# Turning maxima and gate sums from tiles of 128 columns, and a new order of the first steps

## The chip, the cores and the metric

The kernel runs on one core of one Trainium2 chip. The metric is the device time of one execution in microseconds; the median of three timed runs counts. The engines are named as in the profile: PE multiplies matrices (PEld loads its stationary operand, the weights), DVE, ACT and POOL work on vectors, SP issues most of the transfers. Each engine and each queue works its instructions off in order; between engines, semaphores keep the order of the data.

## The reference, cut to what matters

```python
def _attn_ref(q, k, v, proj):            # 4 x 8 heads, 768 tokens, 64 wide; 6 hash bits
    q_bits = (np.einsum('bhsd,dk->bhsk', q, proj) > 0).astype(np.int64)
    k_bits = (np.einsum('bhsd,dk->bhsk', k, proj) > 0).astype(np.int64)
    mask = q_bucket[:, :, :, None] == k_bucket[:, :, None, :]
    scores = scale * np.matmul(q, k.transpose(0, 1, 3, 2))
    scores = np.where(mask, scores, -1000000000.0)
    scores = scores - np.max(scores, axis=-1, keepdims=True)
    attn = np.exp(scores)
    attn = attn / (np.sum(attn, axis=-1, keepdims=True) + 1e-09)
    return np.matmul(attn, v).astype(np.float32)

def _moe_ref(x, w_gate, w1, w2, capacity):   # x: 4 x 768 x 512, capacity 128
    scores = np.einsum('bsd,d->bs', x, w_gate)
    for b in range(B):
        top_idx = np.argpartition(-scores[b], capacity)[:capacity]
        ye = np.maximum(x[b, top_idx] @ w1, 0.0) @ w2
        g = 1.0 / (1.0 + np.exp(-scores[b, top_idx]))
        out[b, top_idx] = x[b, top_idx] + g[:, None] * ye
    return out
```

Queries and keys fall into buckets by the signs of six projections; a query attends to the keys of its bucket. Of each batch's 768 tokens the 128 with the largest gate sums go through a small network.

## The kernel before, in words

The whole program is one list of steps, ORDER (lines 44 to 172). A step is a name with numbers, as `mx.5.1.2`; the loop at L1014 calls the function of that name, which issues its instructions. Each engine gets its instructions in the order in which the list names them, and a semaphore wait is set by what was listed before. The string BANKS says which of four PSUM tiles each step takes that asks for one: big (L260) gives 1024 columns, two banks, one (L263) gives 512. One more bank holds the sums av.

One head h (32 of them) goes through these steps.

- X loads q and k with the 64 features on partitions, xh and xl split them into two 16-bit parts, h or hx multiplies by the projections (32-bit for heads 0 to 3), sg or sx takes the signs. For head 0 the signs are taken straight from PSUM (hash_direct L331, signs_direct L342): hx is one tile of two banks, half e of the tokens in bank e, and sx.0.i.e reads half e for i, queries or keys.
- pa, ps and pb place the parts in the tiles A (queries and keys with their sign rows) and B, as transfers on SP, of which da, dd and xq are the forms for head 0. kd takes differences of key thirds (halves in head 0).
- mx, re and rd find each query's maximum: max_unit (L523) adds a product to a PSUM tile, re makes it non-negative on ACT, then the next product is added, and rd takes the largest on DVE.
- mq (max_clamp, L554) clamps the maxima of all 768 queries into a tile of 128 x 6 in 16 bits; mt (max_turn, L559) turns that on PE into 6 x 128; mc copies it out on DVE; mr places it as a row of A by a transfer. Heads 0 and 1 go another way: mk clamps (clamp_part, L575), mu (row_turn, L581) multiplies each single column with the identity, and mv copies the row.
- s (L619 and L622) multiplies keys by queries in five units, e takes the exponential on ACT, r the low part on DVE, a (L703) multiplies by the values, six steps of 18 products each; w puts the first sums into av, rc and n divide.

After eight heads of a batch, sc sums x times the gate weights on DVE into one column for each 128 tokens (score, L738; the tile of the second half of the features is sct[b, 1], 128 x 6 in 32 bits). tp (turn_scores, L788) turns it to 6 x 128 on PE, ty, ts and sb spread it over the partitions. For the last batch bp (L770) does that on PE in two halves of one PSUM tile, and bc (L783) copies the halves, bc.0 on ACT and bc.1 on DVE. lt, ow, cl, cw and se count ranks, ip, ix and ga gather the chosen tokens, tx, hi and lo turn them, up, hh, hl and dn are the network, fi and sr write back.

wa (warm_av, L658) multiplies a tile of ones by itself into columns of av that nobody reads: its first number is a label, its second the count. init_rest (L287) fills constants on POOL; i0 fills the tile of ones, iv fills constant columns of V and W. wa.0.30 stands near the head of the list.

Of the kernel before, what the change touches and what calls it, by code (L numbers as in the profile page):

```python
# [59 lines left out]
mx.5.1.0 re.5.1.0 re.4.1.1 a.2.4 mx.4.0.2 wl.0.1 rd.4.0 mx.5.0.0 a.2.5 mx.4.1.2 s.3.0 rc.2 rd.4.1 vh.2 n.2 re.5.0.0  # L60
vs.3 mx.5.1.1 e.3.0 X.12 re.5.1.1 s.3.2 e.3.2 wl.0.0 ps.6.0 pb.4.2 w.3 xl.10 X.9 mq.4 mt.4 mc.4 ps.7.0 vw.3 pb.4.3
s.3.1 pb.6.2 mx.5.0.1 pb.6.3 pb.5.0 e.3.1 mx.5.1.2 wt.1 pa.7.1 vl.2 s.3.3 xh.9 s.3.4 mr.4 e.3.3 r.3.0 xh.11 pa.7.0
a.3.0 a.3.1 V.4 kd.6 mx.6.0.0 pb.7.2 r.3.1 X.13 a.3.2 a.3.3 pb.6.0 xl.9 pb.4.1 e.3.4 re.5.0.1 mx.5.0.2 r.3.2 xl.11
pb.7.3 a.3.4 re.6.0.0 a.3.5 wh.1 xh.12 rd.5.0 rd.5.1 wl.1.1 ps.7.1 lg mx.6.0.1 h.2.0.4 mq.5 re.6.0.1 sg.2.0.4 pb.5.1
ws.3 wc.3 mx.6.1.0 re.6.1.0 mt.5 mc.5 pa.8.0 xl.12 X.14 mr.5 X.15 xh.13 rc.3 mx.6.0.2 rd.6.0 vs.4 mx.6.1.1 s.4.0
ps.8.0 re.6.1.1 mx.6.1.2 rd.6.1 e.4.0 pb.6.1 xl.13 s.4.2 s.4.3 s.4.4 vh.3 e.4.2 pa.8.1 n.3 vr.2 sc.0.0.0 e.4.3 w.4
s.4.1 e.4.1 pb.7.1 ps.8.1 r.4.0 s.5.0 mq.6 sc.0.0.1 e.4.4 s.5.2 kd.7 r.4.1 a.4.0 a.4.1 e.5.0 po.0 pb.7.0 mx.7.0.0
mx.7.1.0 re.7.0.0 re.7.1.0 mt.6 a.4.2 a.4.3 vl.3 r.4.2 V.5 mc.6 mr.6 sc.0.0.3 mx.7.0.1 mx.7.1.1 pb.8.2 e.5.2 a.4.4
a.4.5 re.7.1.1 kd.8 re.7.0.1 sc.0.0.4 s.5.1 e.5.1 wl.1.0 pa.9.0 pb.8.3 rc.4 s.5.3 mx.7.0.2 wt.2 pa.9.1 ps.9.1 s.5.4
pa.10.0 vw.4 n.4 pb.9.2 mx.7.1.2 r.5.0 r.5.1 pa.10.1 w.5 vs.5 a.5.0 a.5.1 pb.9.3 e.5.3 rd.7.0 rd.7.1 e.5.4 xh.14 s.6.0  # L70
e.6.0 mx.8.1.0 r.5.2 re.8.1.0 vr.3 X.16 ps.9.0 s.6.2 a.5.2 mq.7 e.6.2 ps.10.0 vw.5 a.5.3 a.5.4 a.5.5 rc.5 wh.2 xl.14
vh.4 mt.7 mc.7 mx.8.0.0 re.8.0.0 mr.7 n.5 r.6.0 pb.8.1 vl.4 s.6.1 sc.0.0.5 w.6 mx.8.1.1 re.8.1.1 pb.9.0 pb.9.1 kd.9
vr.4 wl.2.1 mx.8.0.1 V.6 a.6.0 ws.4 a.6.1 re.8.0.1 wl.2.0 mx.8.0.2 mx.8.1.2 pb.8.0 wc.4 e.6.1 xh.15 rd.8.0 rd.8.1 mq.8
r.6.1 s.6.4 s.7.0 ps.10.1 X.17 e.7.0 s.6.3 pb.10.2 e.6.3 pb.10.3 s.7.2 e.7.2 lc pa.11.1 mx.9.0.0 a.6.2 mt.8 mc.8 vs.6
mr.8 pa.11.0 a.6.3 e.6.4 wt.3 re.9.0.0 s.7.1 ps.11.1 s.7.3 s.7.4 pa.12.1 e.7.1 pb.11.2 pb.11.3 mx.9.1.0 r.6.2 r.7.1
pb.10.0 pb.10.1 e.7.3 mx.9.0.1 re.9.1.0 a.6.4 a.6.5 mx.9.1.1 r.7.0 xl.15 X.18 rc.6 re.9.0.1 n.6 xh.16 xl.16 mx.9.0.2
rd.9.0 s.8.0 re.9.1.1 mx.9.1.2 rd.9.1 mq.9 w.7 a.7.0 s.8.2 e.7.4 e.8.0 sc.0.0.2 xh.17 a.7.1 kd.10 mt.9 mc.9 e.8.2
pb.11.1 a.7.2 r.7.2 a.7.3 ws.5 kd.11 mr.9 wh.3 wc.5 X.21 mx.10.0.0 re.10.0.0 s.8.1 e.8.1 ps.11.0 r.8.0 a.7.4 mx.10.0.1
re.10.0.1 wl.3.1 pa.12.0 X.19 a.7.5 rc.7 n.7 wl.3.0 vh.5 xl.17 s.9.0 mx.10.0.2 e.9.0 w.8 rd.10.0 s.8.3 e.8.3 vl.5
mx.10.1.0 re.10.1.0 sc.0.1.0 wt.4 h.3.0.4 V.7 s.8.4 e.8.4 pa.13.1 pa.13.0 sg.3.0.4 vw.6 ps.12.1 sc.0.1.3 r.8.1 s.9.2  # L80
pb.12.3 a.8.0 mx.10.1.1 a.8.1 e.9.2 sc.0.1.2 mx.11.1.0 r.8.2 re.10.1.1 re.11.1.0 mx.11.0.0 re.11.0.0 sc.0.1.5
mx.10.1.2 rd.10.1 sc.0.1.4 po.1 a.8.2 s.9.1 xh.18 mx.11.0.1 mq.10 e.9.1 re.11.0.1 ps.13.1 a.8.3 vr.5 mt.10 sc.0.1.1
a.8.4 mc.10 mr.10 tp.0 ty.0 ts.0 ps.12.0 r.9.0 ps.13.0 pb.11.0 a.8.5 rc.8 n.8 wh.4 mx.11.1.1 sb.0 pb.12.2 vs.7 vw.7
mx.11.0.2 rd.11.0 re.11.1.1 s.9.4 s.9.3 pb.13.2 pb.13.0 mx.11.1.2 rd.11.1 mq.11 w.9 a.9.0 r.9.1 pa.14.0 e.9.3 e.9.4
# [971 lines left out]
```

## Time and profile before

| | |
|---|---|
| median of three runs | 391.91 us (391.43 to 393.45) |
| profiled execution, as timed | 390.71 us |
| its span, first to last instruction | 388.9 us |
| PE busy | 375.6 us (97%), 5693 instructions |
| PEld busy | 283.1 us (73%) |
| ACT busy | 305.7 us (79%) |
| DVE busy | 299.4 us (77%) |
| POOL busy | 136.4 us (35%) |
| PE's granted clock, mean | 0.994 |

A matmul's end in the profile is modelled and overlaps the next one's start; how long one holds PE is read from the distance of two starts. "Idle before" is the time for which the engine had nothing to do ahead of an instruction, with the instruction that ended it.

### The profile page before, as it was taken

The page shows a single profiled execution, that of the slowest core. Times are in us where ns is not written, and L with a number is a line of the kernel's source. Part 1 is how long each engine was busy: PE and PEld are TensorE (multiplying, and loading weights), DVE is VectorE, ACT ScalarE, POOL GpSimd, SP SyncE. Part 2 cuts the span into 40 slices and gives each one's busy share as a digit, 9 for nine tenths or more (in the row PEclk, how much of TensorE's full clock was granted, in tenths as well). Part 3 has the DMA queues.
Part 4 walks back from the last instruction along what each step waited for, and adds up shares of the span by engine and source line. Part 5 has one row for each costly group of instructions (what it writes and reads, how often), then busy time and mean ns, then how long its engine had stood idle before and what let it go on. Part 6 is the DMA issues. An engine that isn't in the chain of part 4 may idle for free.

```text
span 388.9 us, 13665 instructions
## 1 busy us (share of the span) xinstructions
PE 375.6 (97%) x5693; PEld 283.1 (73%) x5700; DVE 299.4 (77%) x666; ACT 305.7 (79%) x416; POOL 136.4 (35%) x154
## 2 busy tenths in 40 slices
...
GB/s 193 189 221 211 184 189 252 229 166 184 206 240 120 128 201 177 170 158 206 117 185 139 122 156 170 63 100 91 88 103 163 57 117 93 4 3 83 30 29 54
DMA packets 33850, 54.33 MB, mean 140 GB/s; under 512 B 5443, under 2 KB 25137, under 8 KB 33788
## 3 DMA queue, kind: packets, MB, share of 16 engines
...
q14 instruction: 17, 0.14, 0.1%
...
## 4 chain that ended last, share of the span: by engine, by line
PE 78%; DVE 7%; DMA 4%; ACT 4%; issue 3%; SPq 2%; POOLq 0%; POOL 0%; ACTq 0%; DVEq 0%
PE av L703 24%; PE s L619 14%; PE s L622 13%; PE mx L536 13%; PE hp L955 5%; PE yp L986 3%; ACT mx L544 2%; PE h L378 2%; DMA A<-XH 2%; DMA X<-in_qk_dram 1%; DVE cm L811 1%; PE mt L561 1%; DMA out_dram<-xe,idx 1%; PE av L662 1%; DVE jk L749 1%
## 5 line engine op out<-in xcount | busy, mean ns | idle before, releaser
L635 ACT ACTIVATE P<-s 128x1024 int32<-128x1024 f32 (+1 forms) x160 | 145.9, 943 | 21.9 <-PE s L622 20.7
L703 PE MATMUL av<-V,P 128*128 128x65 f16 (+1 forms) x2304 | 120.2, 193 | 0.0
L703 PEld LDWEIGHTS <-P 128*128 128x128 f16 x2304 | 114.9, 97 | 6.7 <-issue 1.0
L619 PE MATMUL s<-A 97*128 97x256 f16 (+1 forms) x384 | 118.3, 326 | 0.8 <-DVE mr L565 0.3
L622 PE MATMUL s<-B 128*128 128x256 f16 (+1 forms) x384 | 117.8, 326 | 0.0
L703 PE MATMUL av<-VR,R 128*128 128x65 f16 x1152 | 116.2, 192 | 0.0
L544 ACT ACTIVATE mx<-mx 128x512 f32<-128x512 f32 (+2 forms) x127 | 98.8, 801 | 18.2 <-PE mx L536 15.6
L703 PEld LDWEIGHTS <-R 128*128 128x128 f16 x1152 | 105.3, 98 | 0.1
L649 DVE TENSOR_SCALAR R<-P 128x1536 f16<-128x1536 uint16 x96 | 92.8, 982 | 10.0 <-ACT P L635 9.5
L410 POOL TENSOR_TENSOR XL<-X,XH 128x768 f16<-128x768 f32 x31 | 50.9, 1646 | 66.2 <-DMA B<-XL 19.0
L552 DVE TENSOR_REDUCE m<-mx 128x2 f32<-128x512 f32 (+1 forms) x65 | 60.4, 952 | 17.2 <-PE mx L536 11.9
L536 PEld LDWEIGHTS <-A 82*128 82x128 f16 x570 | 49.9, 97 | 21.3 <-issue 6.3
L536 PE MATMUL mx<-kd,A 82*128 82x256 f16 (+1 forms) x378 | 59.4, 273 | 2.0 <-DVE kd L510 1.1
L622 PEld LDWEIGHTS <-B 128*128 128x128 f16 x384 | 37.6, 98 | 20.1 <-issue 1.3
L619 PEld LDWEIGHTS <-A 97*128 97x128 f16 x384 | 37.4, 97 | 19.6 <-issue 0.6
...
L536 PE MATMUL mx<-A 82*128 82x256 f16 (+1 forms) x192 | 31.3, 276 | 0.8 <-ACT mx L544 0.6
L481 POOL TENSOR_TENSOR vs<-Vf 128x384 f32<-128x384 f32 x16 | 17.9, 1118 | 34.8 <-DMA Vf<-in_v_dram 34.7
L399 ACT CAST XH<-X 128x768 f16<-128x768 f32 x32 | 26.7, 837 | 2.4 <-DMA X<-in_qk_dram 2.4
L955 PE MATMUL hp<-xth,w1l 128*128 128x128 f16 x128 | 22.2, 219 | 0.0
L955 PE MATMUL hp<-xth,w1h 128*128 128x128 f16 x128 | 22.2, 219 | 0.0
L955 PE MATMUL hp<-xtl,w1h 128*128 128x128 f16 x128 | 22.2, 219 | 0.0
...
## 6 DMA issues: line engine op xcount, KB each, us to landing
...
A<-sg SPq DMA_DIRECT2D x62, 27.0 KB
```

The lines of the kernel that those rows point to most:

```text
L399: nc.scalar.copy(xh, st["X", h])
L410: turn(nc.gpsimd.tensor_tensor(**rest_x(h)))
L481: nc.gpsimd.tensor_tensor(y, t[:, 0:3], t[:, 3:6], op=ALU.add)
L536: nc.tensor.matmul(p[:, t - t0], a[0:KM, 0, t * P : (t + 1) * P], keys, start=first, stop=True, skip_group_check=True,)
L544: nc.scalar.activation(p, p, AF.Relu)
L552: nc.vector.reduce_max(st["m", h][:, t0:t1], max_tile(h, g), axis=AX.X)
L619: nc.tensor.matmul(p[:, o : o + n], a[:, 1, c * P : (c + 1) * P], a[:, 0, q0 : q0 + n], start=True, stop=False,)
L622: nc.tensor.matmul(p[:, o : o + n], bt[:, 1, c * P : (c + 1) * P], bt[:, 0, q0 : q0 + n], start=False, stop=True,)
L635: nc.scalar.activation(pp[:, c0 : c0 + k, q0 : q0 + w], p[:, : k * w].rearrange("p (c q) -> p c q", c=k), AF.Exp, bias=PB * float(np.log(2 ...
L649: mine(nc.vector.tensor_scalar(r, pp.bitcast(U16)[:, :, 0::2], 2.0 ** -24, None, op0=ALU.mult,))
L703: nc.tensor.matmul(o[:, t, 0:n], l, r, start=False, stop=last and l is lo, skip_group_check=True,)
L955: nc.tensor.matmul(o, l[:, k, fs], st[r, b][:, xs], start=(j == 0 and k == 0 and n == 0), stop=(k == 3 and n == 2), skip_group_check=True,)
```

## The change

The tiles of the clamped maxima are made 128 x 128 (16 bits, two buffers, filled with zeros once by init_rest), of which the clamp writes the first six columns; mt turns all 128 columns into 128 rows, of which mc copies the first six as before. The second tile of gate sums is made 128 x 128 in 32 bits in the same way, for tp. mu is left as it was, on single columns of the wider tile.

In the list, wa.0.30 becomes wa.0.34, and wa.1.12, wa.2.6 and wa.3.8 are added between the first steps on PE. The first two signs (sx.0.1.0 and sx.0.0.0) are listed ahead of the second half of hx; i0 is listed ahead of iv.0, and iv.1 comes to the head of the list. The rest of the list has the same steps in another order, mostly moved by a few places on their engines, and BANKS is made anew for it; tiles keep their sizes. Of the list, the diff below shows the head, the places around mt.2 and pb.30.3, and the last batch's comparisons.

```diff
--- before.py
+++ after.py
@@ -42,141 +42,140 @@
 ROWS = (0, 1)
 
 ORDER = """
-iv.0 i0 wa.0.30 lp x0.0 hx.0.0 it x0.1 hx.0.1 X.1 xh.0 dd.0.0.0 da.0.1.0 i1 sx.0.1.0 sx.0.0.0 l6 sx.0.1.1 xh.1
-sx.0.0.1 X.2 xq.0.1 X.3 ia.0 h.0.1.2 kd.0 mx.0.0.0 da.0.1.1 re.0.0.0 mx.0.2.0 re.0.2.0 xl.1 pa.1.1 xq.0.0 pa.1.0
-sg.0.1.2 mx.0.1.0 mx.0.0.1 rd.0.0 mx.0.2.1 V.0 ps.1.0 re.0.1.0 mx.0.1.1 xh.2 xh.3 xl.2 rd.0.2 h.0.2.4 rd.0.1 ps.1.1
-kd.1 da.0.0.1 V.1 vh.0 mx.1.0.0 mk.0.0 vs.0 sg.0.2.4 ia.1 mu.0.0 re.1.0.0 pb.1.3 pa.2.1 mv.0.0 mx.1.1.0 vr.0 mk.0.1
-X.6 pb.1.2 pa.3.0 mx.1.0.1 re.1.1.0 mx.1.1.1 vl.0 s.0.0 mu.0.1 zb vw.0 mv.0.1 re.1.0.1 re.1.1.1 mx.1.0.2 rd.1.0 ps.2.1
...
-e.1.0 pa.5.1 ia.3 a.0.4 a.0.5 mx.2.1.2 rd.2.0 rd.2.1 mq.2 xh.7 e.1.4 pb.2.1 pa.4.0 s.1.2 rc.0 n.0 xl.7 X.10 mx.3.1.0
-e.1.2 re.3.1.0 mt.2 mc.2 mr.2 s.1.1 mx.3.0.0 mx.3.1.1 e.1.1 pb.3.1 h.1.0.4 r.1.0 w.1 a.1.0 a.1.1 re.3.1.1 mx.3.1.2
...
-pb.30.2 pa.31.1 re.30.0.0 a.27.0 ws.15 pa.31.0 s.28.1 pb.30.3 pb.31.2 mt.29 mc.29 a.27.1 a.27.2 e.28.1 mx.30.0.1
...
-sc.3.1.3 a.31.4 a.31.5 rc.31 sc.3.1.1 up.1.4 up.1.5 hh.1.0 tx.2 sl up.1.6 up.1.7 hi.2 hh.1.1 hl.1.0 bp.0 bp.1 n.31
-bc.0 bc.1 hl.1.1 ow.3.0 ow.3.3 ow.3.1 lt.3.0 dn.1.0 dn.1.1 lo.2 dn.1.2 dn.1.3 dn.1.4 dn.1.5 dn.1.6 cl.3.0 up.2.0
...
+lp i0 wa.0.34 iv.0 x0.0 iv.1 x0.1 it hx.0.0 i1 X.1 l6 dd.0.0.0 X.2 X.3 sx.0.1.0 xh.0 xq.0.1 sx.0.0.0 hx.0.1 wa.1.12
+da.0.1.0 sx.0.1.1 sx.0.0.1 xh.1 kd.0 h.0.1.2 sg.0.1.2 ia.1 xq.0.0 V.0 da.0.1.1 mx.0.0.0 re.0.0.0 mx.0.2.0 wa.2.6
+re.0.2.0 pa.1.1 ia.0 pa.1.0 mx.0.0.1 xl.1 rd.0.0 ps.1.1 xh.2 mx.0.1.0 re.0.1.0 ps.1.0 da.0.0.1 V.1 pb.1.2 X.6 xl.2
+mx.0.2.1 wa.3.8 rd.0.2 mx.0.1.1 rd.0.1 h.0.2.4 kd.1 mx.1.0.0 pa.2.1 pa.2.0 mk.0.1 mk.0.0 sg.0.2.4 xh.3 mu.0.0 mv.0.0
+mu.0.1 mv.0.1 vs.0 vh.0 re.1.0.0 pb.1.0 mx.1.1.0 re.1.1.0 ps.2.1 pb.1.3 mx.1.0.1 vl.0 vr.0 re.1.0.1 mx.1.1.1 re.1.1.1
...
+re.2.0.0 kd.3 mx.2.1.1 ia.4 e.1.3 a.0.3 ia.2 mx.2.0.1 re.2.0.1 re.2.1.1 s.1.4 e.1.4 r.0.2 s.1.0 e.1.0 xl.5 xh.7
+mx.2.0.2 xl.4 X.8 pa.4.0 mx.2.1.2 rd.2.0 rd.2.1 mq.2 pa.4.1 a.0.4 a.0.5 s.1.2 pb.2.0 rc.0 mt.2 e.1.2 mc.2 pb.2.1
...
+mx.31.1.1 re.31.1.1 a.28.5 r.29.0 pb.31.2 pb.31.1 rc.28 n.28 mx.31.0.1 sc.3.0.5 s.29.1 re.31.0.1 pb.30.3 pb.31.3 w.29
+sc.3.0.1 mx.31.1.2 e.29.1 s.29.3 e.29.3 pb.31.0 mr.30 vl.15 mx.31.0.2 rd.31.0 a.29.0 s.29.4 rd.31.1 e.29.4 mq.31
...
+hl.1.0 a.31.5 up.1.4 up.1.5 up.1.6 up.1.7 sc.3.1.1 rc.31 sl tx.2 n.31 hh.1.1 hl.1.1 bp.0 bc.0 hi.2 bp.1 bc.1 ow.3.0
+ow.3.5 lt.3.0 ow.3.2 dn.1.0 dn.1.1 lo.2 dn.1.2 dn.1.3 ow.3.4 lt.3.1 dn.1.4 dn.1.5 cl.3.0 cw.3.0 dn.1.6 cl.3.1 up.2.0
...
@@ -289,6 +288,9 @@
         nc.gpsimd.memset(zs, DS * VS)
         nc.gpsimd.memset(acc, 0.0)
         nc.gpsimd.memset(oneb, 1.0)
+        for i in range(2):
+            nc.gpsimd.memset(wide(f"mqi{i}"), 0.0)
+        nc.gpsimd.memset(sums(1, "sci"), 0.0)
 
     def init_a(i):
         done("ia", i)
@@ -551,14 +553,17 @@
         t0, t1 = groups(h)[g]
         nc.vector.reduce_max(st["m", h][:, t0:t1], max_tile(h, g), axis=AX.X)
 
+    def wide(name):
+        return sb.tile([P, P], F16, tag="mq", name=name, bufs=2)
+
     def max_clamp(h):
         need(*(("md", h, g) for g in range(len(groups(h)))))
-        m = st["mq", h] = sb.tile([P, NC], F16, tag="mq", name=f"mq{h}", bufs=2)
-        nc.vector.tensor_scalar(m, st["m", h], FLOOR, 1.0 / MS, op0=ALU.max, op1=ALU.mult)
+        m = st["mq", h] = wide(f"mq{h}")
+        nc.vector.tensor_scalar(m[:, :NC], st["m", h], FLOOR, 1.0 / MS, op0=ALU.max, op1=ALU.mult)
 
     def max_turn(h):
         p = st["mt", h] = one(f"mt{h}").bitcast(F16)
-        nc.tensor.transpose(out=p[:NC, :P], in_=st["mq", h], identity=ident16)
+        nc.tensor.transpose(out=p[:, :P], in_=st["mq", h], identity=ident16)
 
     def max_copy(h):
         mr = st["mr", h] = sb.tile([NC, P], F16, tag="mr", name=f"mr{h}", bufs=2)
@@ -575,7 +580,7 @@
     def clamp_part(h, g):
         need(*(("md", h, i) for i, (a, b) in enumerate(groups(h)) if a // 4 == g))
         t = part(g)
-        m = st["mq", h, g] = sb.tile([P, NC], F16, tag="mq", name=f"mq{h}_{g}", bufs=2)
+        m = st["mq", h, g] = wide(f"mq{h}_{g}")
         nc.vector.tensor_scalar(m[:, t], st["m", h][:, t], FLOOR, 1.0 / MS, op0=ALU.max, op1=ALU.mult)
 
     def row_turn(h, g):
@@ -735,6 +740,9 @@
 
 
 
+    def sums(i, name):
+        return sb.tile([P, P if i else NC], F32, tag=f"sc{i}", name=name, bufs=1)
+
     def score(b, i, t):
 
         f = 2 * b + i
@@ -742,7 +750,7 @@
         need(*(("n", 4 * f + j) for j in range(n // D)))
         done("sc", b, i, t)
         if ("sct", b, i) not in st:
-            st["sct", b, i] = sb.tile([P, NC], F32, tag=f"sc{i}", name=f"sc{b}_{i}", bufs=1)
+            st["sct", b, i] = sums(i, f"sc{b}_{i}")
         if i:
             need(("sc", b, 0, t))
         jk = sb.tile([P, DM], BF16, tag="jks", name=f"jk{b}_{i}_{t}", bufs=1)
@@ -764,7 +772,7 @@
         )
         nc.vector.reduce_sum(sc, xw, axis=AX.X)
         nc.vector.tensor_tensor(sc, sc, st["rc", h], op=ALU.mult)
-        nc.vector.tensor_tensor(sc, sc, st["sct", B - 1, 1], op=ALU.add)
+        nc.vector.tensor_tensor(sc, sc, st["sct", B - 1, 1][:, :NC], op=ALU.add)
         st["sct", B - 1, 1] = sc
 
     def spread_last(e):
@@ -788,7 +796,7 @@
     def turn_scores(b):
         need(*(("sc", b, 1, t) for t in range(NC)))
         p = st["tp", b] = one(f"tp{b}")
-        nc.tensor.transpose(out=p[:NC, :P], in_=st["sct", b, 1], identity=ident)
+        nc.tensor.transpose(out=p[:, :P], in_=st["sct", b, 1], identity=ident)
 
     def copy_scores(b):
         t = st["scT", b] = sb.tile([NC, P], F32, tag="scT", name=f"scT{b}", bufs=1)
```

## Rows read from the trace of the kernel before

**Rows 1.** page, the chain that ended last: shares by engine, by line
```profile
PE 78%; DVE 7%; DMA 4%; ACT 4%; issue 3%; SPq 2%; POOLq 0%; POOL 0%; ACTq 0%; DVEq 0%
```

**Rows 2.** stretches: us, then PE, PEld, DVE, ACT, POOL busy, clock, DMA, GB/s
```profile
10.00:15.00 5.00, 4.46 (x19) 1.34 (x16) 4.00 (x5) 4.87 (x7) 4.73 (x4) 0.68 0.61 183
80.00:120.00 40.00, 39.56 (x622) 30.31 (x619) 31.90 (x70) 38.12 (x53) 19.45 (x21) 1.00 0.65 189
360.00:370.00 10.00, 9.37 (x138) 7.59 (x139) 6.71 (x26) 1.20 (x2) 1.38 (x2) 1.00 0.11 29
```

**Rows 3.** instructions of L561: ns min/median/max, first and last start
```profile
L561 PEld LDWEIGHTS <-mq x30: 81/81/82, 34.2 to 333.5; 128*6 128x6 f16 x30
```

**Rows 4.** timeline of PE at 102 us: start, us, instruction, idle before
```profile
102.29 0.20 PE L703 MATMUL av<-VR,R 128*128 128x65 f16 x1
102.41 0.22 PE L561 MATMUL mt<-c,mq 128*6 128x128 f16 x1
102.56 0.24 PE L703 MATMUL av<-V,P 128*128 128x65 f16 x2
```

**Rows 5.** timeline of PE at 199.8 us
```profile
199.73 0.19 PE L703 MATMUL av<-VR,R 128*128 128x65 f16 x1
199.76 0.27 PE L791 MATMUL tp<-cs,sc 128*6 128x128 f32 x1
199.87 0.22 PE L955 MATMUL hp<-xth,w1h 128*128 128x128 f16 x1
199.93 0.22 PE L955 MATMUL hp<-xtl,w1h 128*128 128x128 f16 x1
```

**Rows 6.** timeline of PE at 26 us
```profile
25.88 0.27 PE L586 MATMUL mu<-c,mq 128*1 128x128 f16 x2
26.09 0.20 PE L703 MATMUL av<-V,P 128*128 128x65 f16 x1
```

**Rows 7.** timeline at 33 us, DVE and PE
```profile
33.02 1.09 DVE L557 TENSOR_SCALAR mq<-m 128x6 f16<-128x6 f32 x1
...
34.16 0.22 PE L561 MATMUL mt<-c,mq 128*6 128x128 f16 x1 [0.86 <-DVE rc L713]
```

**Rows 8.** chain that ended last, in order of time, 70 to 100 us
```profile
81.88 4.29 DMA X<-in_qk_dram
```

**Rows 9.** timeline of PE at 355 us
```profile
354.76 0.82 PE L778 MATMUL bp<-cs,sc 128*128 128x128 f32 x6
```

**Rows 10.** timeline of the first steps, PE and DVE
```profile
1.63 3.08 PE L662 MATMUL av<-ones 128*128 128x116 f16 x30 [1.63 <-POOL ones L282]
...
4.64 1.64 PE L336 MATMUL hx<-X,pjt 128*32 128x384 f32 x8
...
6.34 2.76 DVE L347 TENSOR_SCALAR A<-hx,pjt 18x384 f16<-18x384 f32 x4 [1.12 <-PE hx L336]
...
6.91 1.48 PE L378 MATMUL h<-X,pjt 128*32 128x384 f32 x4 [0.63 <-DMA X<-in_qk_dram]
...
9.53 0.81 PE L536 MATMUL mx<-kd,A 82*128 82x384 f16 x4 [1.14 <-DVE kd L510]
...
11.55 2.69 DVE L552 TENSOR_REDUCE m<-mx 128x2 f32<-128x768 f32 x3 [0.97 <-ACT mx L544]
...
13.04 2.56 PE L378 MATMUL h<-X,pjt 128*32 128x384 f32 x8
...
17.15 0.70 DVE L598 CAST A<-mu 1x512 f16<-1x512 f32 x1
```

**Rows 11.** who waited for whom, whole run: us, times, longest
```profile
DVE sbc L785 <- ACT sbc L785: 1.2, 1, 1.2
```

**Rows 12.** page, costliest groups: busy us, mean ns | idle before
```profile
L703 PEld LDWEIGHTS <-P 128*128 128x128 f16 x2304 | 114.9, 97 | 6.7 <-issue 1.0
...
L399 ACT CAST XH<-X 128x768 f16<-128x768 f32 x32 | 26.7, 837 | 2.4 <-DMA X<-in_qk_dram 2.4
```

**Rows 13.** who waited for whom, first 45 us
```profile
PEld L586 <- DVE mq L579: 0.6, 2, 0.4
```

More of the change, by code (lines that the diff above doesn't have):

```diff
@@ L60 @@
[L60 to L84, printed above, removed]
@@ new lines @@
+pb.5.0 mr.4 V.4 mx.5.0.1 s.3.4 a.3.0 xh.9 xl.9 e.3.3 e.3.4 r.3.2 a.3.1 a.3.2 re.5.0.1 X.13 mx.6.0.0 a.3.3 pb.7.3
+re.6.0.0 mx.5.0.2 rd.5.0 pb.7.2 wh.1 a.3.4 xl.11 a.3.5 wl.1.1 pb.6.0 rc.3 pb.5.1 xh.12 mx.6.0.1 lg re.6.0.1 rd.5.1
+mq.5 ws.3 wc.3 h.2.0.4 sg.2.0.4 xl.12 mx.6.1.0 ps.7.1 X.14 vs.4 mt.5 mc.5 mx.6.0.2 re.6.1.0 mx.6.1.1 xh.13 s.4.0 mr.5
+n.3 re.6.1.1 X.15 e.4.0 vh.3 xl.13 s.4.2 ps.8.1 e.4.2 ps.8.0 pa.8.1 w.4 mx.6.1.2 rd.6.0 rd.6.1 pa.8.0 r.4.0 s.4.1
+s.4.3 e.4.1 s.4.4 s.5.0 e.4.3 e.5.0 sc.0.0.0 e.4.4 kd.7 a.4.0 sc.0.0.4 a.4.1 mq.6 mx.7.0.0 re.7.0.0 vl.3 po.0 V.5
@@ new lines @@
+a.6.0 pb.9.3 a.6.1 V.6 re.8.1.1 wl.2.1 re.8.0.1 mx.8.1.2 mx.8.0.2 rd.8.0 ps.10.0 rd.8.1 wc.4 e.6.1 xh.15 s.6.4 pb.9.1
+s.7.0 e.7.0 wl.2.0 kd.9 s.6.3 s.7.2 e.6.3 r.6.1 X.17 e.7.2 e.6.4 pa.11.1 vr.4 pa.11.0 mx.9.0.0 re.9.0.0 a.6.2 a.6.3
+sc.0.0.1 mq.8 mt.8 mc.8 s.7.1 e.7.1 pb.10.3 pb.10.2 vs.6 s.7.3 pb.9.2 e.7.3 mr.8 pb.10.1 mx.9.0.1 mx.9.1.0 wt.3
+re.9.1.0 r.6.2 r.7.0 ps.11.1 r.7.1 re.9.0.1 ps.11.0 a.6.4 a.6.5 rc.6 n.6 s.7.4 pb.11.2 pb.11.3 X.18 pa.12.1 xl.15
+mx.9.1.1 mx.9.0.2 s.8.0 xh.16 xl.16 re.9.1.1 mx.9.1.2 pb.10.0 w.7 a.7.0 rd.9.0 rd.9.1 mq.9 s.8.2 kd.10 pb.11.0 a.7.1
@@ new lines @@
+a.11.1 s.12.0 r.11.1 a.11.2 pb.15.2 xl.20 rd.13.0 pb.14.0 wl.5.0 e.11.4 e.12.0 s.12.2 e.12.2 s.12.1 e.12.1 rd.13.1
+mq.13 mt.13 a.11.3 mx.14.0.0 re.14.0.0 xh.21 r.11.2 mc.13 vr.6 r.12.0 a.11.4 a.11.5 r.12.1 rc.11 pa.16.0 n.11 ws.7
+mx.14.1.0 re.14.1.0 wc.7 mx.14.0.1 re.14.0.1 ps.15.1 wl.5.1 mr.13 pa.16.1 h.4.0.4 po.2 s.12.3 vs.8 sg.4.0.4 ps.16.0
+mx.14.0.2 vh.7 rd.14.0 mx.14.1.1 xl.21 s.13.0 e.12.3 ps.16.1 s.12.4 pb.16.3 pa.17.0 w.12 gt.0 a.12.0 wt.6 s.13.2
+re.14.1.1 e.12.4 e.13.0 mx.14.1.2 s.13.1 a.12.1 e.13.2 pb.16.2 kd.15 mx.15.0.0 sc.1.0.0 e.13.1 pb.15.0 re.15.0.0
```

194 lines of the change are left out of this document (101 added, 93 removed), and 8 rows, old and new, of the table BANKS.

## Prediction

> **What bounds the kernel now.** I read the chain that ended last first: PE holds 78% of it, and the transpositions of the clamped maxima have 1% of it to themselves, 3.9 us [rows 1]. Then the table by stretches [rows 2]: from 80 to 120 us PE is busy 39.6 of 40 us and ACT 38.1, so ACT is the next engine there. From 10 to 15 us PE has gaps, and its granted clock is 0.68: part of that stretch ran at 1.2 and not at 2.4 GHz. Near the end, from 360 to 370 us, 0.6 us of PE is open. So from some 40 us on, a change is worth what it takes off PE's own sequence; before that, what it takes off a chain through DVE, ACT and PE; and the gaps that a better list could close are as small as 0.4 us in those 40. The sum is made against the profiled execution: span 388.9 us, 390.71 us as timed; the median is 391.91, 1.2 us above that.
>
> **Turning from 128 columns.** Each of the heads 2 to 31 has one turn (max_clamp, max_turn): thirty, each behind a weight load of 6 columns [rows 3]. What one costs PE is read from starts. In [rows 4] the product ahead of it starts at 102.29, the turn at 102.41, the next product at 102.56. Products with 65 columns follow each other by 0.03 us (199.73 to 199.76 in [rows 5]), and one with 128 columns holds PE for 0.06 (199.87 to 199.93). So the turn is 0.12 - 0.03 = 0.09 us late and what follows it 0.15 - 0.06 = 0.09 late: PE runs empty before and after. The same shows where a plain 16-bit product has a weight tile of one column [rows 6]: two of those hold PE from 25.88 to 26.09, 0.21 and not 0.11 us, so it is not the transposing. A 32-bit turn from 6 columns has none of it: 0.03 before it, 0.11 of its own [rows 5]. No row shows a 16-bit turn from 128 columns. Its bounds are the 16-bit product with 128 weight columns (0.06, nothing lost) and today's turn (0.24); I take 0.06, because weight width is what all 16-bit rows that drain have in common. Saved per turn: 0.18, thirty times: 5.4 us. Two turns also wait for the clamp (34.16 is one [rows 7]) and save only their second half; that takes off 0.2. Not all the rest reaches the end. Eight turns lie between 45 and 118 us, where ACT is 95% busy and the chain passes through transfers as long as 4.29 us [rows 8]; I let half of these eight, 0.7 us, be taken back. Term: -4.5 us, from -3.7 (all eight taken back) to -5.4.
>
> The clamp still writes 6 columns and the copy still reads 6 rows, so DVE pays nothing more. The columns beyond are zeroed once on POOL, three fills more in init_rest; POOL's first real wait is then for the first halves of x, and nothing else reads these tiles before DVE's first clamp behind the reductions at 11.55 [rows 10]: nothing.
>
> **Gate sums.** Three 32-bit turns from 6 columns hold PE 0.11 us each [rows 5]; six 32-bit ones with 128 columns take 0.82 us with the drain of the last, starting 0.11 apart [rows 9]. Nothing, within 0.2 us.
>
> **The first steps.** Four edits meet here.
> (a) ones16 is filled ahead of the fills of V and W on POOL, so the first products start sooner than 1.63 [rows 10]; four more at 0.10 us each (30 in 3.08) take 0.4 us, which that start pays. Nothing.
> (b) First signs. Today they start at 6.34, when both halves of hx are done (4.64 + 1.64 = 6.28), though the first two read only the first half. That ends near 5.7 (an estimate: 4.64, one pair at half clock, 0.6, and 0.49, the length of a last product in [rows 10]). Listed ahead of hx.0.1 the signs can start there, 0.6 us sooner. But now hx.0.1 is listed behind two signs that read the same PSUM tile. Whether it must wait for them is shown by the other tile with two halves: DVE's copy of the second half of bp waited 1.2 us for ACT's copy of the first [rows 11], so a tile is guarded whole. Then the signs, 0.69 us each (2.76 for four), end at 7.1; hx.0.1 runs 7.15 to 7.95; the other two signs end at 9.4 instead of 9.1. The 12 products behind hx.0.1 and the four of h.0.1.2 (1.48 us) follow on PE, 7.8 to 9.85, so the first product on a difference, at 9.53 now, comes near 9.8. Behind it the new order of mx.0.0.1 ahead of mx.0.1.0 gives 0.3 back, and xh.2, a cast of 0.84 [rows 12] now ahead of re.0.1.0 on ACT, delays the third reduction, by 0.5 on DVE's sequence, which decides the first scores: it is full from the reductions at 11.55 to the copy of the maxima at 17.15 to 17.85, and the scores follow that. They start some 0.45 us later. Then mu.0.1, which today waits behind them for DVE, 0.4 us [rows 13], stands ahead of them: 0.4 back.
> (c) Constant products: 26 more, at 0.10 us by [rows 10] at the lower clock, half that (an estimate by the two levels) at the upper: 1.3 to 2.6 us. They lie in PE's waits for the second x, for re and for the third reduction; where one of these is gone they cost their length, in (b) already for the 12.
> (d) The clock. The products of h at 13.04 run at half clock: eight in 2.56 us, where four at full clock took 1.48 at 6.91; pairs start 0.64 instead of 0.32 apart, 1.3 us in all. Should the clock stay up, PE is ready sooner, but DVE is not, and of the 1.3 us only up to 0.4 reach the end.
> Sum of the start: zero, from -0.9 (a second half that does not wait: signs 0.6 sooner and not 0.3 later) to +1.1 (the 12 products at the lower clock, 0.6 more, and none of the 0.4 back).
>
> **The rest of the list.** One stall is large enough to name: the first turn waits 0.86 us for a clamp that took 1.09 [rows 7]. In the new order the last two value steps of head 0 (36 products of 0.03 us, 1.1 us) stand between the maxima and that turn. The stall goes: -0.7, from 0 to -0.9. At the end bp.1 is listed behind bc.0 and, by the rule of the whole tile, makes PE wait for ACT, some 0.6 us; the comparisons then start about 0.6 us sooner, and there are 0.6 us of holes in 360 to 370 [rows 2] for that to close: nothing, within 0.7. Elsewhere steps move by three places on PE and on SP, two on DVE, one on ACT. I take nothing for it, within 1 us, since the holes are no larger.
>
> Sum: -4.5 + 0 + 0 - 0.7 = -5.2 us. 390.71 becomes 385.5; from the median 391.91 it is **386.7**.
>
> **Rivals.**
> First, the turn keeps its drain, because it is a 16-bit transposition and not because of its width. For: no row shows a wide one. Against: the plain products of [rows 6] drain too. It gives 391.91 - 0.7 = 391.2.
> Second, PE's gain is given back in the middle: ACT at 95% and SP's queue set the pace for all 13 turns up to 160 us (13 times 0.18, 2.3 us, of which 0.7 is counted), and the start is 0.6 late. For: ACT's share. Against: PE's own 99%. 386.7 + 1.6 + 0.6 = 388.9.
> Third, slower: the wide load stands open ahead of each turn, and the drain stays. Its place is the thirty turns, its price a load of 128 columns at 97 ns [rows 12], thirty times, 2.9 us; it decides as soon as the drain does not go, and gives 391.2 + 2.9 = 394.1. Against: the load of 6 columns already takes 81 ns [rows 3], and wide loads lie under the product ahead. The Trainium skill (TensorE: Matmul & The Clock Gate, LDWEIGHTS) has a rule on this side: a load takes as long as it has columns, so 128 cost over twenty times what 6 do. The trace disagrees on the ratio, 97 against 81 ns; by the page alone each turn would grow by 0.1 us and the sum would end near 394.
> Fourth, slower too: a transfer that SP now issues up to 17 places later stands bare. Some 4.3 us each [rows 8]; two of them would be 8.6 - 5.2, 395.3. Against: the move that leaves least, pb.30.3, still has two value steps (1.1 us) and score and maxima steps of PE between it and its use.
>
> **How the numbers follow.** Forecast 0.66 (its own range 384.3 to 388.4: 386.7 less 0.9, 0.9, 0.2 and some of the list; plus 0.8, 0.7 and 0.2), drain stays 0.10, given back 0.15, open load 0.04, bare transfers 0.05. The range, 383.8 to 390.6, takes in the second rival and leaves out the others. This kernel is measured to about 0.5%, 2 us: faster (under 389.95) takes the forecast and most of the second rival, 0.77; same, the first and what is left of the second, 0.14; slower, 0.09.
>
> **What would show it.** The turn with a load of 128 columns: its start 0.03 us after a value product, the next one 0.06 after it. In the chain, the turn's line without its 1%. At the start: the first sign near 5.7, hx.0.1 near 7.1 if the whole tile is guarded and near 5.5 if not, the clock between 10 and 15 us. No 0.86 us before the first turn. Wrong if turns still stand 0.09 from both neighbours; if PE's busy share from 60 to 120 us falls while the stretch stays as long (given back); or if PE waits several us on a transfer.

## The result, and the profile after

The changed kernel takes 388.64 us (median of 8 runs, 386.77 to 389.86) beside 392.11 for the kernel before (8 runs on the same chip): a ratio of 0.9897, 95% interval 0.9867 to 0.9927, or 4.0 us less, from 2.9 to 5.2 (the two medians alone lie 3.5 apart). Every ratio here is to the kernel before, run beside it on the same chip. The profiled execution took 388.95 us, with a span of 387.2 (before: 390.71 and 388.9). All line numbers behind this point are those of the kernel that is shown; mt is now L566, the value products L708.

The turn first, on PE at 104 us (start, length, instruction), the answer to [rows 4]:

```profile
104.38 0.20 PE L708 MATMUL av<-VR,R 128*128 128x65 f16 x1
104.42 0.22 PE L566 MATMUL mt<-c,mq 128*128 128x128 f16 x1
104.47 0.22 PE L708 MATMUL av<-V,P 128*128 128x65 f16 x2
```

The turn starts 0.03 us after the product ahead of it and holds PE for 0.055, where it was 0.12 and 0.15. Where nothing is waited for, the other turns hold PE for 0.055 to 0.066 too. Their loads, now of 128 columns, and what still stands ahead of them (the answer to [rows 3]):

```profile
L566 PEld LDWEIGHTS <-mq x30: 95/96/98, 35.3 to 331.5; 128*128 128x128 f16 x30
...
its engine sat idle before it (us, times) until:
  DVE mq L562: 4.2, 8
```

A load of 128 columns takes 96 ns beside 81 for six, and lies under the product ahead. Some turns do wait for the clamp on DVE; the row counts PE and its loads together, and PE itself stands 1.4 us, at the turns of heads 5 and 10. Now the stretches of [rows 2] and the first steps of [rows 10]:

```profile
10.00:15.00 5.00, 4.75 (x28) 2.13 (x27) 2.26 (x4) 2.31 (x4) 3.23 (x2) 0.77 0.20 52
80.00:120.00 40.00, 39.16 (x630) 30.23 (x629) 33.13 (x66) 37.63 (x53) 20.52 (x21) 1.00 0.68 202
360.00:370.00 10.00, 10.00 (x128) 7.55 (x125) 3.79 (x13) 1.68 (x3) 1.95 (x2) 1.00 0.16 50
```

```profile
0.99 3.47 PE L667 MATMUL av<-ones 128*128 128x116 f16 x34 [0.99 <-POOL V L301]
4.39 1.34 PE L338 MATMUL hx<-X,pjt 128*32 128x384 f32 x4
7.65 0.84 PE L338 MATMUL hx<-X,pjt 128*32 128x384 f32 x4 [1.92 <-DVE A L349]
8.42 0.98 PE L667 MATMUL av<-ones 128*128 128x116 f16 x12
9.33 2.77 PE L380 MATMUL h<-X,pjt 128*32 128x384 f32 x4
12.03 0.92 PE L538 MATMUL mx<-kd,A 82*128 82x384 f16 x4
...
20.82 0.38 PE L624 MATMUL s<-A 97*128 97x512 f16 x1
```

From 80 to 120 us PE gets 630 products done instead of 622 and is busy 39.16 us instead of 39.56. From 360 to 370 it has no hole left. At the start hx.0.1 waits 1.92 us for the signs of the first half, and in this execution the clock fell early: h.0.1.2 at 9.33 took 2.77 us, not 1.48. The stretch around it, columns as in [rows 2], with a granted clock of 0.50, 1.2 GHz:

```profile
8.85:12.26 3.41, 3.41 (x12) 0.96 (x10) 1.50 (x4) 0.20 (x1) 1.89 (x2) 0.50 0.56 168
```

The first score product (L624) comes at 20.82; before it came at 17.94.

To see where time goes, I cut each execution at four rows: the first score product, the reciprocal of head 10 and that of head 31 on DVE, and the start of the last product. These are the rows of before, then the last three of the changed kernel:

```profile
17.94 0.38 PE L619 MATMUL s<-A 97*128 97x512 f16 x1
138.99 0.19 DVE L715 RECIPROCAL rc<-rc 128x6 f32<-128x6 f32 x1
352.24 0.19 DVE L715 RECIPROCAL rc<-rc 128x6 f32<-128x6 f32 x1
383.34 0.38 PE L986 MATMUL yp<-w2h,hth 128*128 128x512 f16 x1
```
```profile
140.49 0.19 DVE L720 RECIPROCAL rc<-rc 128x6 f32<-128x6 f32 x1
350.44 0.19 DVE L720 RECIPROCAL rc<-rc 128x6 f32<-128x6 f32 x1
381.58 0.38 PE L994 MATMUL yp<-w2h,hth 128*128 128x512 f16 x1
```

The distances between them, in us, one profiled execution each (the lower kernels are those of the experiments below):

| kernel | first scores | to head 10 | head 10 to 31 | to last product |
|---|---|---|---|---|
| before | 17.94 | 121.05 | 213.24 | 31.11 |
| changed | 20.82 | 119.66 | 209.95 | 31.14 |
| changed, run again | 18.49 | 120.52 | 210.23 | 31.14 |
| turn alone | 19.02 | 123.58 | 209.88 | 31.11 |
| list alone | 18.33 | 121.15 | 213.14 | 31.14 |
| own tiles for hx | 17.47 | 120.36 | 209.99 | 31.14 |
| ..., bp.1 ahead of the copy | 17.77 | 120.27 | 209.58 | 30.38 |

Between head 10 and 31 the change saves 3.0 to 3.3 us. Up to head 10 it saves 0.5 to 1.4, at the start it loses 0.6 to 2.9, and at the end nothing moves. The first column also holds the landing of x, which differs between executions: DVE's first cast of x starts at 4.66 us before, at 5.65 in the changed kernel, at 4.86 when it was run again, and at 5.76 with the turn alone.

### The profile page after: what moved, and what is told of

It is laid out like the page before. It is cut to its first block, busy times and chain, and to the rows that moved or that the text cites. A ratio compares the mean times of both kernels' runs of the same rounds, so it can differ in the third digit from the quotient of the medians.

```text
span 387.2 us, 13730 instructions
## 1 busy us (share of the span) xinstructions
PE 372.9 (96%) x5730; PEld 285.5 (74%) x5730; DVE 301.7 (78%) x666; ACT 305.1 (79%) x416; POOL 138.8 (36%) x157
## 4 chain that ended last, share of the span: by engine, by line
PE 77%; ACT 8%; DVE 6%; issue 5%; DMA 2%; POOLq 0%; SPq 0%; DVEq 0%; ACTq 0%
PE av L708 23%; PE s L624 14%; PE s L627 14%; PE mx L538 13%; PE hp L963 4%; PE yp L994 4%; ACT mx L546 3%; ACT P L640 3%; PE h L380 2%; DVE R L654 1%; DVE m L554 1%; DMA X<-in_qk_dram 1%; DMA out_dram<-xe,idx 1%; DVE sg L393 1%; ACT V L462 1%
## 5 line engine op out<-in xcount | busy, mean ns | idle before, releaser
L624 PE MATMUL s<-A 97*128 97x256 f16 (+1 forms) x384 | 118.4, 326 | 1.1 <-DVE mr L570 0.3
L708 PEld LDWEIGHTS <-P 128*128 128x128 f16 x2304 | 115.3, 97 | 5.5 <-issue 0.3
L708 PE MATMUL av<-V,P 128*128 128x65 f16 (+1 forms) x2304 | 119.3, 193 | 0.0
L708 PE MATMUL av<-VR,R 128*128 128x65 f16 x1152 | 115.6, 192 | 0.1
L708 PEld LDWEIGHTS <-R 128*128 128x128 f16 x1152 | 105.2, 98 | 0.2 <-DVE R L654 0.2
L654 DVE TENSOR_SCALAR R<-P 128x1536 f16<-128x1536 uint16 x96 | 94.8, 999 | 9.4 <-ACT P L640 9.3
L624 PEld LDWEIGHTS <-A 97*128 97x128 f16 x384 | 37.4, 97 | 19.1 <-issue 0.8
L483 POOL TENSOR_TENSOR vs<-Vf 128x384 f32<-128x384 f32 x16 | 16.9, 1053 | 28.6 <-DMA Vf<-in_v_dram 28.5
```

Of the source, the lines that this page charges most:

```text
L483: nc.gpsimd.tensor_tensor(y, t[:, 0:3], t[:, 3:6], op=ALU.add)
L624: nc.tensor.matmul(p[:, o : o + n], a[:, 1, c * P : (c + 1) * P], a[:, 0, q0 : q0 + n], start=True, stop=False,)
L654: mine(nc.vector.tensor_scalar(r, pp.bitcast(U16)[:, :, 0::2], 2.0 ** -24, None, op0=ALU.mult,))
L708: nc.tensor.matmul(o[:, t, 0:n], l, r, start=False, stop=last and l is lo, skip_group_check=True,)
```

## The experiments

**The turn alone**, in the list of before, gate sums from six columns; and **the list alone**, with the turn from six columns.

The edit of the first, cut to the turn itself (the tiles are widened and filled as in the change):

```diff
...
-        nc.tensor.transpose(out=p[:NC, :P], in_=st["mq", h], identity=ident16)
+        nc.tensor.transpose(out=p[:, :P], in_=st["mq", h], identity=ident16)
...
```

> The list of the kernel before, with the clamped maxima turned from tiles of 128 columns and nothing else changed (gate sums narrow, no further constant products). Theory A, the turns carry the gain and the new list gives some of it back at the start: PE loses 0.18 us less at each of 30 turns, 386.5 to 387.5 us, a ratio of 0.985 to 0.989, at or below the changed kernel. Theory B, the list carries the gain and the turns only move PE's waits: 391 to 392 us, ratio 0.997 to 1.001.

> The kernel before with the new list, its constant products and its PSUM places, and with the narrow turns of before (maxima and gate sums). Theory A: the start is 1 us late and the rest of the list brings nothing, 392 to 394 us, ratio 1.001 to 1.005. Theory B: 388 to 390 us, ratio 0.990 to 0.995.

The turn alone took 388.43 us beside 391.79 (ratio 0.991, 0.9879 to 0.9942); the list alone 392.83 (ratio 1.0033, 1.0008 to 1.0058). So the turn carries the gain and the list alone costs about a microsecond. The table says the same of the turn: 209.88 us from head 10 to 31 with it, 213.14 with the list. Of the list's microsecond the profiled execution shows 0.4, all ahead of the first scores; where the rest lies is not shown. Nor do the two add up: -3.4 and +1.0 us alone, -4.0 together (the changed kernel run again on this chip, below). Beside wide turns the list is 0.6 us better, not worse, but these intervals overlap, so its price there stays open.

The turn's 123.58 us to head 10 hold a wait and a stretch at half clock behind it (the waits of PE from 60 to 75 us, then that stretch, columns as in [rows 2]):

```profile
PE s L627 <- DMA B<-A: 1.7, 1, 1.7
```
```profile
68.75:72.16 3.41, 3.20 (x13) 1.85 (x14) 1.23 (x3) 1.72 (x2) 2.09 (x2) 0.50 0.76 220
```

That is some 3 us, and what was saved up to there is gone in that execution. The list alone shows what became of the stall that the prediction meant to lose. Who waited for whom on PE, 20 to 125 us, before and then with the list alone:

```profile
PE mt L561 <- DVE rc L713: 0.9, 1, 0.9
```
```profile
PE mt L560 <- DVE mq L556: 1.7, 2, 1.1
```

The 0.9 us at head 2 are gone (the profile names rc, which DVE works off right behind the clamp), and the turns of heads 5 and 10 wait 1.7 us for their clamps instead, where before they waited 0.3.

**A tile for each half of hx**, with the changed kernel run again beside it.

```diff
-        if e == 0:
-            st["hx", h] = big(f"hx{h}")
-        hp = st["hx", h]
+        hp = st["hx", h, e] = one(f"hx{h}_{e}")
...
```

> The changed kernel, but with a PSUM tile of its own for each half of the first head's projections, so that the second half has no signs to wait for. Theory A, the start's loss reaches the end: the second half follows the first at once, the first product on a difference comes 1 to 2 us sooner, and the end 0.5 to 1.5 us sooner, 387 to 388.2 us. Theory B, later waits swallow it: first scores sooner, the end unchanged at 388.6 us.

> The changed kernel unchanged, beside the three others on the same chip: 388.6 us, ratio 0.987 to 0.993. Every theory expects the same; it is the mark for the others.

386.77 us (ratio 0.9881, 0.9844 to 0.9917) and 387.80 (0.9893, 0.986 to 0.9927). The intervals overlap; the profiles tell more. PE's first steps with own tiles:

```profile
4.39 1.53 PE L336 MATMUL hx<-X,pjt 128*32 128x384 f32 x8
5.86 0.78 PE L665 MATMUL av<-ones 128*128 128x116 f16 x12
6.96 1.48 PE L378 MATMUL h<-X,pjt 128*32 128x384 f32 x4 [0.32 <-DMA X<-in_qk_dram]
```

All eight products of hx stand in one row and h starts at 6.96; in the changed kernel run again hx.0.1 waited till 6.85 and h started at 8.34. The first scores came 1.0 us sooner, and the lead is still there at the last product, by then 1.4. So a tile of two banks is guarded as a whole. Not all of the 1.0 is the guard's, since x landed 0.25 us sooner. From DVE's first cast of x to the first scores it takes 12.7 to 13.4 us in the seven kernels here with own tiles and the constant products, and 13.6 to 13.9 in the three executions with one tile and the clock up: the guard costs 0.3 to 1.1 us.

**How wide must the turn be?** Two kernels give each head another width; the edit of the first:

```diff
-        nc.tensor.transpose(out=p[:, :P], in_=st["mq", h], identity=ident16)
+        w = (6, 32, 64, 96, 112, 127, 128)[h % 7]
+        nc.tensor.transpose(out=p[:w, :P], in_=st["mq", h][:, :w], identity=ident16)
...
```

It also turns the three tiles of gate sums from 6, 64 and 128 columns. The second, made from the kernel with bp.1 ahead of the copy (below), takes 65, 72, 80 or 88.

> The changed kernel, but the turn of head h takes 6, 32, 64, 96, 112, 127 or 128 columns by the rest of h divided by 7, and the three turns of gate sums take 6, 64 and 128 columns. Read: the distance from the start of the product ahead to the turn's, and from the turn's to the next, where nothing waits. Theory (a full weight tile of 128 columns is what spares PE the drain): 0.12 + 0.15 us for all widths from 6 to 127, 0.03 + 0.06 for 128 only. Rival one (the drain shrinks with the columns that are missing): 0.12 + 0.15 at 6, about the middle at 64, near 0.03 + 0.06 at 127. Rival two (any width from some lower one on is enough): a step somewhere between 32 and 112. Gate sums in 32 bits: no drain at any width by all three; the wide one costs the next product 0.14 us instead of 0.11, the 64-column one lies between. Time: by the theory three sevenths to six sevenths of the gain of the turns goes, some 391 us; by rival two between that and 388.

> The kernel with bp.1 ahead of the copy; the turn of head h takes 65, 72, 80 or 88 columns by the rest of h divided by 4. From the runs so far 64 columns drain (0.12 + 0.18 us) and 96 don't (0.03 + 0.06). Theory (one column over half of 128 is enough): none of the four drains, and the time is that of 128 columns, 385.6 within 1.2. Rival (96 columns are the first that do): all four drain, as 64 does, and 3 us are lost, 388 to 389. Second rival: a step in between. No forecast of the place rests on anything but the two widths measured.

From starts of single rows, behind a value product (0.03 us to the next where nothing drains):

| columns | 6 | 32 | 64 | 65 | 80 | 96 | 127 | 128 |
|---|---|---|---|---|---|---|---|---|
| product ahead to turn, ns | 122 | 121 | 121 to 125 | 29 | 29 | 29 | 29 | 29 |
| turn to next, ns | 150 | 163 | 176 | 57 | 63 | 70 | 83 | 55 |

```profile
102.74 0.20 PE L709 MATMUL av<-VR,R 128*128 128x65 f16 x1
102.86 0.24 PE L567 MATMUL mt<-c,mq 128*64 128x128 f16 x1
103.04 0.23 PE L709 MATMUL av<-V,P 128*128 128x65 f16 x2
```
```profile
171.39 0.19 PE L707 MATMUL av<-VR,R 128*128 128x65 f16 x1
171.42 0.22 PE L565 MATMUL mt<-c,mq 128*65 128x128 f16 x1
171.48 0.27 PE L623 MATMUL s<-A 97*128 97x256 f16 x1
```

The drain goes between 64 and 65 columns, on both sides at once. My theory of a full tile, of the first text, is wrong; its rival of a step was right, and so was the second text's theory that one column over half is enough. Times agree: 389.05 us for the first kernel, in which thirteen of the thirty turns drain (nine of the nineteen between head 10 and 31, where it took 211.47, 1.6 us over 209.9, and nine times 0.18 is 1.6), and 385.38 for the second, in which none does (385.62 for the kernel that it is made from, shown below). The 32-bit turns of gate sums start 29 ns after the product ahead at 6, 64 and 128 columns, and the next product 109, 110 and 141 ns after them: no drain at any width, so the step is one of the 16-bit products.

Above 64 columns the distance to the next product still grows, from 57 ns to 83, and falls back to 55 at full width. The weight loads of the first kernel rise and fall likewise, mean ns the second number:

```profile
L567 PEld LDWEIGHTS <-mq 128*127 128x127 f16 x4 | 0.5, 134 | 1.7 <-DVE mq L562 1.5 <-DVE idx L873 0.2
L567 PEld LDWEIGHTS <-mq 128*64 128x64 f16 x5 | 0.5, 106 | 0.8 <-DVE mq L562 0.4 <-DVE rc L719 0.2
...
L567 PEld LDWEIGHTS <-mq 128*128 128x128 f16 x4 | 0.4, 97 | 0.2 <-DVE mq L562 0.2
```

**Without the 26 constant products** between the first steps, on the kernel with own tiles (wa.1.12, wa.2.6 and wa.3.8 taken out of the list).

> The changed kernel with a tile for each half of hx, without the 26 constant products that stand between the first steps (wa.1.12, wa.2.6, wa.3.8); the 34 at the head stay. Theory (they lie in waits and buy nothing that reaches the end): first scores and the end stay within 0.4 us of the kernel with them, 386.8 us; PE's granted clock still falls once in the first 20 us, as it does with them. Rival (they keep the clock up): without them the half-clock stretch is there and with them it is not, and the first scores come over 1 us later, 388 us at the end. Second rival (they stand on the path, 0.10 us each where the clock is low): without them the first scores come 0.6 to 1.3 us sooner.

387.41 us (ratio 0.9882, 0.9861 to 0.9904): no difference that these runs can tell. The clock does differ: the mean granted clock is 0.984 to 0.991 in its four runs, 0.992 to 1.000 in the six with the products, and 0.994 to 0.998 in ten runs of two other kernels with them on the same chip. In its profile a stretch at half clock fell on h.0.2.4:

```profile
13.89:17.30 3.41, 3.41 (x18) 1.14 (x12) 3.04 (x6) 2.05 (x3) 2.94 (x6) 0.50 0.89 256
```

So the products keep the clock up more often, as the rival said, and in time that is worth between nothing and a microsecond here (first scores 18.65 against 17.47 to 19.00 in the seven with own tiles and with them).

**bp.1 ahead of the copy bc.0**, on the kernel with own tiles.

```diff
-... hh.1.1 hl.1.1 bp.0 bc.0 hi.2 bp.1 bc.1 ow.3.0
+... hh.1.1 hl.1.1 bp.0 bp.1 bc.0 hi.2 bc.1 ow.3.0
```

> The changed kernel with a tile for each half of hx, and bp.1 listed directly behind bp.0, ahead of ACT's copy bc.0, as the kernel before has it. Theory (bp.1 behind the copy makes PE wait 0.73 us on the tile that is guarded whole, and the holes that this closes later are as large): PE's 0.7 us wait at bp.1 goes, the holes of the last 30 us grow by about as much, and the end moves by less than 0.4 us from 386.8. Rival (the wait is a loss): the end comes 0.7 us sooner, 386.1. Second rival (the copy sooner is a gain of its own): 0.5 or more later, 387.3.

385.62 us (ratio 0.9854, 0.9829 to 0.9879). From head 31 to the last product it takes 30.38 us instead of 31.14: the first rival's 0.7. PE has no stall left in that stretch. In the changed kernel PE stands there, on the tile that is guarded whole:

```profile
352.96 0.49 PE L786 MATMUL bp<-cs,sc 128*128 128x128 f32 x3
354.02 0.54 PE L786 MATMUL bp<-cs,sc 128*128 128x128 f32 x3 [0.57 <-ACT sbc L793]
```

**Where the early turns' gain goes.** In three of the kernels with own tiles ACT waits 1.8 to 2.5 us near 65 us for one transfer of x, X.13 (in the profiled execution of the changed kernel it does not). Three kernels list other transfers behind it; the first named the wrong one, as the text of the second tells.

> The changed kernel with a tile for each half of hx, and four steps listed later: the second weight tile's transfer (wt.1, 512 KB) behind X.13 instead of ahead of X.9, its casts (wh.1 on ACT, wl.1.1 on POOL) behind xh.14, and V.4 (384 KB) behind X.9. Theory (the gain of the turns is given back at 63 to 67 us because X.9 lands late behind 900 KB of other transfers in one queue, ACT then waits 2.5 us for it and PE 1.8 us for ACT): ACT's wait before the cast of X.9 falls from 2.46 us to under 0.8, PE's stall near 67 us from 1.79 to under 0.5, the reciprocal of head 10 comes 1 us or more sooner than 137.8, and the end comes 0.7 to 1.5 us sooner, 385.3 to 386.1. Rival (ACT itself is full there, so what PE gains comes back as another wait on ACT between 70 and 120 us whatever lands when): the wait goes but the reciprocal of head 10 stays within 0.4 us of 137.8, and the end within 0.5 of 386.8.

> The kernel with bp.1 ahead of the copy, and V.4 (384 KB) and wt.1 (512 KB) listed directly behind X.13, with the casts of wt.1 (wh.1, wl.1.1) behind xh.14. The run before this meant to do so and named the wrong transfer: ACT waits for X.13, not X.9, so that edit moved V.4 sooner, not later, and X.13 was issued at 62.8 and not at 58.3 us; it then took 3.3 us to its cast instead of 6.9. Theory (the gain of the turns is given back at 63 to 67 us because X.13 stands in the queue behind these 900 KB): X.13 is issued at 57 to 58 and in place 3.3 us later; ACT's wait of 1.8 us before its cast falls under 0.3; PE's holes from 60 to 80 us fall from 1.9 to under 0.8; the reciprocal of head 10 comes at 136.5 to 137.3 instead of 138.0; the end 0.7 to 1.5 us sooner, 384.1 to 384.9. Rival (ACT, or transfers as a whole, set the pace from 40 to 120 us, so another wait takes its place): the wait is gone, the reciprocal of head 10 stays within 0.4 us of 138.0, the end within 0.5 of 385.6. Second rival (something else then comes late, as in the run before): the end over 0.5 us later.

> The kernel with bp.1 ahead of the copy, and V.4 (384 KB) alone behind X.13; the weight tile wt.1 and its casts stay. X.13 is then issued one transfer sooner with 384 KB less ahead of it. Theory (what stands ahead of X.13 sets the wait): ACT's wait before its cast falls from 1.8 to near 0.5 us, less than with both moved; holes of PE from 60 to 80 us under 1.3; the end 0.3 to 0.8 us sooner than 385.6. Rival (another wait takes its place): the end within 0.3 us.

The first took 388.79 us (ratio 0.9928, 0.9908 to 0.9948): V.4 went ahead, X.13 was issued 4 us later, and PE waited 1.5 us for a row of maxima (mr). The other two took 385.84 (0.9831, 0.9798 to 0.9863) and 386.04 (0.9837, 0.9803 to 0.9872). ACT's casts around X.13, without the move and with both transfers moved:

```profile
60.78 0.86 ACT L399 CAST XH<-X 128x768 f16<-128x768 f32 x1
65.19 0.83 ACT L399 CAST XH<-X 128x768 f16<-128x768 f32 x1 [1.79 <-DMA X<-in_qk_dram]
```
```profile
60.77 0.85 ACT L399 CAST XH<-X 128x768 f16<-128x768 f32 x1
64.24 0.82 ACT L399 CAST XH<-X 128x768 f16<-128x768 f32 x1
```

ACT's wait is gone; with V.4 alone moved, 0.9 us of it stay. PE's idle time from 60 to 80 us only falls from 1.2 to 1.1 (busy 18.82 and 18.90 of 20), since another transfer is late next:

```profile
PE s L622 <- DMA A<-mr: 0.8, 1, 0.8
```

To head 10 it takes 119.40 us instead of 120.27, but the kernel of the second widths has the old place of X.13 and takes 119.55, with a wait of 0.6 for it. So executions of one list differ by as much as the move brings, and its worth stays open; the wait did turn into another, as the rival had it.

**The first eleven turns narrow again** (heads 2 to 12), to see what they bring at all.

```diff
-        nc.tensor.transpose(out=p[:, :P], in_=st["mq", h], identity=ident16)
+        w = NC if h <= 12 else P
+        nc.tensor.transpose(out=p[:w, :P], in_=st["mq", h][:, :w], identity=ident16)
```

> The kernel with bp.1 ahead of the copy, but the eleven turns of heads 2 to 12 take 6 columns again, as in the kernel before; those of heads 13 to 31 take 128. What do the first eleven bring? Read from the reciprocal of head 10 less the first scores (120.3 us with all turns wide, 121.05 before) and from the end. The prediction's own step (a few of them given back): the eleven are worth 2.0 us on PE and some 1.3 of it at the end, so 386.9 us here and 121.6 us to head 10. Rival (given back wholly, since transfers and ACT set the pace to head 10): the end within 0.4 us of 385.6, 120.3 to 120.7 to head 10. Second rival (nothing given back): 387.6 and 122.3. From head 10 to head 31 all three expect 209.6 to 210.0 us, as with all wide, against 213.2 before.

387.53 us (ratio 0.9865, 0.9841 to 0.9888), 1.7 us above the kernel with X.13 moved, on the same chip, and 1.9 above its own base on another. To head 10 it took 121.04, against 119.40 to 120.27 in the four kernels with all turns wide and bp.1 ahead. Three more executions with all turns wide, of the changed kernel twice and of own tiles, took 119.66, 120.52 and 120.36. So eleven turns, 2.0 us of PE, bring 0.5 to 1.6 there and 1.5 to 2.2 by the times on this chip (387.53 beside 385.84, 386.04 and the one run of the second widths, 385.38). Given back wholly does not fit: it asked for an end within 0.4 of 385.6. How much comes back stays open, since the ratio lies only 0.0011 above that of the base, with overlapping intervals, and the profiles are one execution each.

## Why the prediction was right, and where not

The forecast of 386.7 us was 1.9 too low; faster was right. The time is in the range, but 0.2 above the forecast's own part of it, which ended at 388.4: the range held because it takes in the second rival. Step by step:

**The drain** was read rightly from starts. 0.03 and 0.055 us stand where I took 0.03 and 0.06, and nineteen turns of 0.18, 3.4 us, arrived as 3.0 to 3.3 between head 10 and 31. That it is the width and not the transposing was right, but 65 columns are enough and 128 are not needed. The Trainium skill (TensorEngine Tiling (Array Packing), Tiling Modes: Available Configurations and Key Properties) states that PE is drained when the tiling mode changes, and lists modes of 128, 64 and 32 columns; the step between 64 and 65 agrees with that, and so do narrow products behind each other, which start 55 ns apart (the last section). That a weight tile's width alone changes the mode is inferred; no run shows a mode. **The early turns** were put at half given back for eight of them; 0.5 to 1.4 of 2.0 us arrived for eleven in the changed kernel's two profiles. Together the turns' term, -4.5, came out as -4.7 and -3.5 from the first scores on, with whatever the list adds there, and as -3.4 in the medians of the turn alone.

**The third rival** (an open load) falls: the drain went, and the load lies under the product ahead. Load times rise from 81 ns at 6 columns to 134 at 127, 0.44 ns a column, and are 97 at 128. The Trainium skill (TensorE: Matmul & The Clock Gate, Weight-path perf modes) says that a faster load is used for exactly 128 columns of a type other than 32 bits; the drop from 134 to 97 agrees. By the rule of the Trainium skill that I weighed (TensorE: Matmul & The Clock Gate, LDWEIGHTS), a column would cost 0.83 ns; the runs show about half of it, on a base of some 78.

**The rest of the list**, -0.7, is the step that failed. The stall of [rows 7] did go; I did not ask which turn is late next, and two clamps that DVE delivers late took 1.7 us instead. Behind the first scores the profile of the list alone is as long as that of before (121.15 and 213.14 us beside 121.05 and 213.24), so the term came out as nothing, with narrow turns; with wide ones it was not measured apart from them.

**The start**, taken at nothing from -0.9 to +1.1, cost 0.4 to 0.6 us where the clock stayed up. The whole-tile guard was as foreseen: hx.0.1 waits, and the first product on a difference, forecast near 9.8, came at 9.58 with the list alone and 9.75 in the changed kernel run again. What I overlooked: on DVE the cast dd stands ahead of the first signs and waits for x. It started at 5.65 us in the changed kernel's profile, so the signs came at 6.24, hardly sooner than 6.34; run again it started at 4.86, and the signs came at 5.44, sooner than the 5.7 that I had. **The clock** was mis-sized: I let 0.4 of 1.3 us reach the end, because I had only seen the stretch at 13 us. Where it falls varies: at 8.85 to 12.26 it hit h.0.1.2, for which the rest waits, and the first scores came 2.3 us later than in the execution run again (0.8 of that is x landing later).

**The gate sums** cost a little: from start to start 142 ns and not 109, three times, 0.1 us. **bp.1 behind the copy** was foreseen as a wait and as nothing in sum against before, and so it is, 31.14 beside 31.11; that the wait could be had back for 0.76 us I did not see.

**The second rival**, 388.9, named nearly the measured time, and its start 0.6 late is near what the runs with the clock up show, but the early gain is not lost wholly. The terms, as they came out, are -3.0 to -3.3 from head 10 on, -0.5 to -1.4 before it, and +0.6 or +2.9 at the start; that is -1.8 us for the profiled execution (390.71 to 388.95) and -3.0 for the one run again (387.75). Against the -5.2 of the forecast, the latter misses 1.0 on the turns, 0.7 on the list and 0.5 at the start. That makes 2.2, as much as the second rival lies above the forecast, from other parts: its number is near by luck. The execution with the early clock fall is the slower of the two, and the medians lie at 388.64 and 387.80.

Two kernels have a median below the changed kernel's: own tiles for hx with bp.1 ahead of the copy, 385.62 us (ratio 0.9854), and the same with X.13 moved, 385.84 (0.9831); their intervals overlap, and each overlaps a little with the changed kernel's when run again (0.986 to 0.9927).
